# First heads' q and k written by column-tile matmuls straight into the padded layout

## The chip, the cores and the metric

One core of a Trainium2 chip. The time is device microseconds of one execution; lower is better. The engines are named as the profile names them: PE (TensorE), DVE (VectorE), ACT (ScalarE), POOL (GpSimd), SP (SyncE, here only an issuer of transfers).

## The reference

Two layers, A and B, run twice in turn over x of 2048 tokens by 640 features, all bfloat16. B is a feed-forward layer. A is causal attention inside four segments of 512 tokens, with 32 heads of 20 features, mixed with a linear-attention memory that runs over the segments.

```python
def _A_ref(x, wq, wk, wv, wo, beta):
    ...
    phi = lambda t: jnp.where(t > 0, t + 1.0, jnp.exp(t))
    g = _sigmoid(beta).reshape(1, H, 1, 1)
    ...
    for s in range(N):
        qs, ks, vs = (q[:, :, s].copy(), k[:, :, s].copy(), v[:, :, s].copy())
        logits = jnp.einsum('bhqd,bhkd->bhqk', qs, ks) * scale + mask
        p = _softmax(logits, axis=-1)
        a_dot = jnp.einsum('bhqk,bhkd->bhqd', p, vs)
        pq = phi(qs)
        num = jnp.einsum('bhld,bhde->bhle', pq, M)
        den = jnp.einsum('bhld,bhd->bhl', pq, z)[..., None] + 1e-06
        a_mem = num / den
        outs.append(g * a_mem + (1.0 - g) * a_dot)
        pk = phi(ks)
        M = M + jnp.einsum('bhld,bhle->bhde', pk, vs)
        z = z + jnp.einsum('bhld->bhd', pk)
    ...
x = x + _A_ref(_layernorm(x, axis=-1), A_wq, A_wk, A_wv, A_wo, A_beta)
x = x + _B_ref(_layernorm(x, axis=-1), B_w1, B_w2)
x = x + _A_ref(_layernorm(x, axis=-1), A_wq, A_wk, A_wv, A_wo, A_beta)
x = x + _B_ref(_layernorm(x, axis=-1), B_w1, B_w2)
```

## The kernel before

**A planner writes the order.** The whole program is a set of Python generators (streams), each of which yields operations, needs and acquisitions of buffers. The planner `Sched` keeps a time for each engine and always emits the operation that its own model lets start first; equal starts are decided by a priority (the number in `S.add`), with scores and exponentials at 0, v at 4, the q and k projections at 5, constants at 7 and loads at 8. Each engine then runs its instructions in that fixed order and waits on semaphores. The table `SHIFT` (from line 175) adds an offset in ns to the start that the planner compares, by stream, phase and count of operations; it changes the order and nothing else.

**TensorE modes.** A projection can be emitted in full width (line 764, 128 output features at once) or as four column tiles of 32 features (line 767). Scores are emitted in row tiles (line 1293). The planner lets a projection keep the column mode that it finds, and chooses anew only behind scores.

**The start.** x, wk and wq are loaded in pieces: the first 256 columns of wk and wq (`wk0`, `wq0`) ahead of the rest, then wv (`loads`, lines 610 to 631). The first segment has four tiles of 128 tokens; each is normalised, transposed on TensorE (`first_tile`, line 847) and copied to xnT. `proj_first` (line 982) then projects q and k by chunks of 128 features (c = 0 to 4; n = 0 is k, n = 1 is q). Chunks 0 and 1 come in three pieces, over tile 0, tile 1, and tiles 2 and 3 together (`PIECES`); chunks 2 to 4 in one piece. Each piece is copied from PSUM to `stg` (lines 971 and 972), where a feature lies on the partition of its place in the chunk.

**The padded layout.** Scores need the four heads of a group at partitions 0, 32, 64 and 96, with 20 features each. `pad` holds this for two groups (a pair, z = 0 and 1), for k and q, over 512 tokens. Usually a chunk goes from stg to scratch in HBM (`spill`, line 1047) and back from there into pad, 20 rows at a time (`fill`, line 1096). For the first pair `first_heads` (line 1065) copies rows straight from stg to pad: nine transfers, on the ACT and SP queues in turn (line 1089). The second pair needs chunks 1 and 2 through the scratch.

**Scores to output.** A pair has five rounds of two halves. Each half is a batch of score matmuls (line 1293) and an exponential on ACT over 128 x 1024 (line 1357); POOL then applies the causal selection (line 1369), and TensorE multiplies with v (line 1389). Four pairs make a segment, 40 exponentials.

**Other pieces that the change touches.** `late_loads` (line 633) loads the x tiles of the third segment (`x2..`, line 637) once the first pair's transfers are issued. `consts` (line 679) builds `maskg`, which picks the blocks of heads in the memory update: selections on POOL, then five multiplications by gate values on DVE (line 727). `phi_` (line 1117) frees or transforms the stg slots. It needs k of chunk 0 in stg; q of the first segment is never transformed.

Of the kernel before, what the change touches and what calls it, by code (L numbers as in the profile page):

```python
# [12 lines left out]
DH = 20  # L13
# [146 lines left out]
class Spawn:  # L160
# [345 lines left out]
def bass_interleave_layers__memory_aug_infini_attn__dense_activation_relu__prompt_kernel(  # L506
    nc, A_x, A_wq, A_wk, A_wv, A_wo, A_beta, B_x, B_w1, B_w2, out,
):
    with contextlib.ExitStack() as es:
# [438 lines left out]
        def proj_part(a, s, c, n, h):  # L948
# [29 lines left out]

            yield Spawn(5, settle())
            return tk  # L980

        def proj_first():
            order = [(c, n, h) for h in range(len(PIECES)) for c in range(2) for n in range(2)]
            order += [(c, n, None) for c in range(2, FC) for n in range(2)]
# [752 lines left out]
```

## Time and profile before

| | us |
|---|---|
| Three runs | 550.38, 552.99, 553.38 (median 552.99) |
| The profiled execution | 550.77 |
| Its span in the profile | 548.3 |
| First score matmul, first exponential | 17.97, 18.40 |

A line of the profile gives the start and the length in us, the engine, the line of the kernel, the operation, and out<-in by the program's names; `x5` means five instructions in a row; square brackets hold the idle time just before and what ended it. "SPq" and "ACTq" are those engines' queues when they issue transfers. "PEld" is the loading of weights on TensorE, which overlaps the matmuls. In tables of stretches each engine has its busy time with the count of instructions, followed by the granted TensorE clock, the DMA share and GB/s. In grouped lines the two numbers behind the bar are the summed busy time in us and the mean ns of one instruction. In lists of waits the three numbers are us in total, times, and the longest.

### The profile page before, as it was taken

How to read it: one execution, taken by the hardware profiler on the slowest of the kernel's cores; microseconds unless marked ns; L12 is line 12 of the kernel's file. 1: busy time of each engine (PE TensorE's matmuls, PEld its weight loads, DVE VectorE, ACT ScalarE, POOL GpSimd, SP SyncE). 2: the span in 40 equal slices, each digit the busy share in tenths (PEclk: the TensorE clock that was granted, in tenths of full speed). 3: DMA queues.
4: the chain of work that ended last, by engine and by line, in shares of the span. 5: the costliest groups of instructions: out<-in, count | busy, mean ns of one | idle time of the engine just before them, and what ended most of it. 6: DMA issues, size and time to landing. Idle time of an engine off the chain costs nothing.

```text
span 548.3 us, 22987 instructions
## 1 busy us (share of the span) xinstructions
PE 540.1 (99%) x10283; PEld 309.9 (57%) x10283; DVE 424.7 (77%) x1060; ACT 409.9 (75%) x522; POOL 196.8 (36%) x305
## 2 busy tenths in 40 slices
PE   8999999999999999999999999999999999999997
PEld 7434465455554555545465554665456655657766
DVE  4999898798889789987798887989688877637102
ACT  6899979899878898788888878886787776551140
POOL 2655533343444334343344444334333322301000
PEclk9999999999999999999999999999999999999999
DMA  8799789845635326375384614571265611340401
GB/s 272 189 231 259 162 179 203 222 86 105 164 83 89 78 39 163 78 114 77 115 144 114 110 31 140 115 126 26 52 179 102 122 34 28 80 83 15 88 4 51
DMA packets 133476, 62.36 MB, mean 114 GB/s; under 512 B 112258, under 2 KB 123266, under 8 KB 133378
## 3 DMA queue, kind: packets, MB, share of 16 engines
q1 hardware_dynamic: 132832, 60.38, 50.8%
q8 instruction: 81, 1.33, 1.0%
q10 hardware_dynamic: 546, 0.52, 0.3%
q14 instruction: 17, 0.14, 0.1%
HBM read 20.57 MB, written 12.85 MB: 61 GB/s over the span
## 4 chain that ended last, share of the span: by engine, by line
PE 89%; DVE 4%; DMA 4%; POOL 1%; ACT 1%; SPq 1%; issue 1%
PE ps L767 48%; PE ps L764 22%; PE ps L1293 9%; PE ps L1389 6%; PE ps L1172 2%; DMA scr<-stg 1%; DMA x_sb<-in_A_x_dram 1%; PE ps L1230 1%; DMA otk<-otu 1%; PE ps L1564 1%; ACT PT L1357 1%; DVE stats L785 1%; POOL PT L1369 1%; SPq L615 0%; POOL rstd L801 0%
## 5 line engine op out<-in xcount | busy, mean ns | idle before, releaser
L1357 ACT ACTIVATE PT<-ps 128x1024 bf16<-128x1024 f32 x320 | 309.3, 1023 | 61.6 <-PE ps L1293 57.6
L1369 POOL TENSOR_SCALAR_AFFINE_SELECT PT<-PT 128x512 bf16<-128x512 bf16 x256 | 169.9, 681 | 247.6 <-ACT PT L1357 247.6
L767 PE MATMUL ps<-xnT,w_r 128*32 128x512 bf16 x1856 | 110.9, 379 | 0.0
L767 PE MATMUL ps<-w_r,hT 128*32 128x320 bf16 (+1 forms) x1876 | 72.7, 295 | 0.0
L767 PEld LDWEIGHTS ps<-xnT,w_r 128*32 128x32 bf16 x1856 | 46.7, 97 | 44.6 <-issue 5.0
L1293 PE MATMUL ps<-pad 20*128 20x512 bf16 (+3 forms) x1024 | 63.3, 301 | 0.0
L764 PE MATMUL ps<-w_r,hT 128*128 128x320 bf16 x376 | 60.3, 300 | 0.0
L1606 DVE TENSOR_TENSOR x_sb<-x_sb,ps 128x320 bf16<-128x320 bf16 (+1 forms) x65 | 30.7, 475 | 37.8 <-PE ps L767 35.6
L785 DVE BATCH_NORM_STATS2 stats<-x_sb 128x6 f32<-128x320 bf16 x124 | 55.2, 474 | 3.9 <-DMA x_sb<-in_A_x_dram 3.3
L767 PEld LDWEIGHTS ps<-w_r,hT 128*32 128x32 bf16 x1876 | 47.9, 97 | 12.4 <-issue 1.6
L1293 PEld LDWEIGHTS ps<-pad 20*128 20x128 bf16 x1024 | 17.8, 92 | 51.1 <-issue 25.0
L764 PEld LDWEIGHTS ps<-w_r,hT 128*128 128x128 bf16 x376 | 34.7, 98 | 17.5 <-issue 5.0
L1587 ACT ACTIVATE hT<-ps 128x512 bf16<-128x512 f32 x52 | 31.1, 598 | 17.9 <-PE ps L767 17.3
L1586 DVE TENSOR_SCALAR hT<-ps 128x512 bf16<-128x512 f32 x52 | 35.3, 680 | 11.7 <-PE ps L767 9.0
L1511 DVE TENSOR_TENSOR x_sb<-x_sb,ps 128x320 bf16<-128x320 bf16 x64 | 30.1, 478 | 15.5 <-PE ps L767 12.1
L801 POOL TENSOR_TENSOR rstd<-lnU,mhalf 128x2 f32<-128x2 f32 (+2 forms) x27 | 21.0, 778 | 56.2 <-DVE lnU L797 42.8
L1389 PE MATMUL ps<-PT,v_aug 128*21 128x128 bf16 (+3 forms) x896 | 40.3, 300 | 0.0
L1399 DVE CAST otu<-ps 128x512 bf16<-128x512 f32 x50 | 34.1, 683 | 7.9 <-PE ps L1389 7.6
L971 DVE CAST stg<-ps 128x512 bf16<-128x512 f32 x42 | 28.5, 683 | 8.4 <-PE ps L767 7.1
L1483 DVE TENSOR_TENSOR o_sb<-otk,rden 128x320 bf16<-128x320 bf16 x62 | 33.9, 571 | 0.6
L831 DVE TENSOR_SCALAR xn_tok<-x_sb,mv,rstd 128x640 bf16<-128x640 bf16 x60 | 29.8, 519 | 3.4 <-POOL rstd L801 3.4
L1138 ACT ACTIVATE stg<-stg 128x512 bf16<-128x512 bf16 x50 | 31.6, 631 | 0.4 <-DVE rtmp L1136 0.4
(113 smaller groups left out, 706.7 us busy)
## 6 DMA issues: line engine op xcount, KB each, us to landing
pad<-scr SPq DMA_DIRECT2D x124, 80.0 KB
scr<-stg SPq DMA_DIRECT2D x34, 256.0 KB, 2.6
out_dram<-x_sb SPq DMA_DIRECT2D x15, 160.0 KB, 2.2
w_r<-in_B_w_dram SPq DMA_DIRECT2D x10, 216.0 KB, 3.8
w_r<-in_B_w_dram SPq DMA_DIRECT2D x13, 160.0 KB, 2.9
x_sb<-in_A_x_dram SPq DMA_DIRECT2D x10, 160.0 KB, 3.3
scr<-w_r SPq DMA_DIRECT2D x5, 256.0 KB, 4.0
wv_r<-in_A_wv_dram SPq DMA_DIRECT2D x1, 800.0 KB, 7.7
```

What stands on the lines that cost most here:

```text
L764: return e.matmul(view(dst.ap, b), a, b, start=(k == 0), stop=(k == last))
L767: return e.matmul(view(dst.ap[rows], b), part, b, start=(k == 0), stop=(k == last))
L785: tk = yield dve(320, 1, lambda e, c2=c2: e.bn_stats(stats6[:, t, c2, :], x_sb[:, t, c2 * 320:(c2 + 1) * 320]), xt)
L1138: te = yield act(512, lambda e, q=q: e.activation(q, q, ACT.Exp), [tr] + p, psum=False)
L1293: fns.append([(lambda e, z=z, j=j, hh=hh, N=N, o=o, sl=sl, q=hh % 2: e.matmul(slot.ap[:, q, o:o + N], sl.ap[32 * hh:32 * hh + DH, z, 0, 12 ...
L1357: tx = yield act(1024, lambda e, dst=dst, src=src: e.activation(dst, src, ACT.Exp, scale=SCALE), sc + pw)
L1369: tm = yield pool(600.0, lambda e, reg=reg: e.affine_select(out=reg, in_=reg, pattern=[[0, 4], [1, 128]], compare_op=ALU.is_ge, fill=0.0, ...
L1389: fns.append((lambda e, OD, j=j, hh=hh: e.matmul(OD.ap[32 * hh:32 * hh + DH + 1, 128 * j:L], VAUG[vx(a, s)][:, j, 4 * g + hh, :], pt.ap[:, ...
L1399: te = yield evac(L, 1, lambda e: e.tensor_copy(dst, OD.ap), lambda e: e.activation(dst, OD.ap, ACT.Copy), [tk] + OTU[0].tks)
L1483: to = yield dve(320, 1, lambda e, z=z, dst=dst: e.tensor_tensor(dst, av[:, z, :, :, 0:DH], rd.ap[:, z].to_broadcast([128, NJ, 4, DH]), AL ...
L1586: th = yield evac(512, 1, lambda e: e.tensor_scalar(hT[:, dc, :], bk.ap[:, :], 0.0, None, ALU.max), lambda e: e.activation(hT[:, dc, :], b ...
L1587: lambda e: e.activation(hT[:, dc, :], bk.ap[:, :], ACT.Relu), [tk] + HT.tks)
```

## The change

Four things change together.

1. k and q of the first eight heads (groups z = 0 and 1) are no longer projected as chunk 0 and copied. A new generator, `padded_part`, projects one group over two tiles: for each of the five blocks of input features, four column-tile matmuls, one a head, each with 32 columns of the weights from the head's first on. The four results lie at partitions 0, 32, 64 and 96 of one PSUM bank, and one copy takes all 128 partitions to pad. The 12 columns above a head's 20 belong to neighbouring heads; nothing reads those rows. There are eight such parts (two groups, k and q, two halves of the tokens).
2. Chunk 1 is still projected to stg, its first two pieces ahead of the padded parts and the third behind them. k of chunk 0 is copied back from pad to stg by seven transfers on SP, q of chunk 0 isn't kept in stg at all, and pad's release waits for the copies back.
3. The third segment's x comes in two transfers on SP right behind wv and beta, instead of four single tiles among the late loads.
4. The masks' memset and selections stand earlier in the stream of constants (ahead of the need of the second pair of normalised tiles), and the five multiplications by the gates go from DVE to POOL. All offsets in `SHIFT` are new (some 260 entries).

```diff
 SHIFT = {
-    (0, 0, 0): -12, (0, 1, 1): -26, (0, 2, 0): -50, (0, 3, 0): -50, (1, 0, 0): -312, (1, 0, 1): -1663,
...
+    (0, 0, 0): -12, (0, 0, 1): -62, (0, 3, 0): -50, (0, 4, 1): -25, (1, 0, 0): 50, (1, 0, 1): -100, (1, 0, 2): -550,
...
 }
@@ loads, behind wv and beta
+            for i in range(0, NJ, 2):
+                t = 2 * NJ + i
+                tk = yield dma("sp", sem_("d_x2%d" % (i // 2)), 327680, lambda e, t=t: e.dma_start(
+                    x_sb[:, t:t + 2, :], xs[:, t:t + 2, :]), lat=2000.0)
+                for k in range(2):
+                    S.set("x2%d" % (i + k), tks=[tk])
@@ late_loads
-            pieces = x_pieces(2)
-            pieces += [rows("wo", wo_r, A_wo, k) for k in range(FC)]
+            pieces = [rows("wo", wo_r, A_wo, k) for k in range(FC)]
@@ consts
-                tm = yield dve(140, 1, lambda e, mc=mc, h0=h0, h1=h1: e.tensor_tensor(
-                    mc, mc, gt[:, 2, h0:h1][:, :, None].to_broadcast([128, h1 - h0, DH]), ALU.mult), [tg] + tmm, port=True)
+                tm = yield pool(500, lambda e, mc=mc, h0=h0, h1=h1: e.tensor_tensor(
+                    mc, mc, gt[:, 2, h0:h1][:, :, None].to_broadcast([128, h1 - h0, DH]), ALU.mult), [tg] + tmm)
@@ new, ahead of proj_first
+        HALF = ((0, 2), (2, 4))
+
+        def padded_part(z, n, h, ev):
+            w_r, nm = ((wk_r, "wk0"), (wq_r, "wq0"))[n]
+            xt = yield Need("xts", 0, 0)
+            xt = xt[0]
+            sl = yield Need("pad00")
+            sl = sl[0]
+            w = yield Need(nm)
+            t = yield Need("xt", 0, 0, h)
+            i0, i1 = HALF[h]
+            t0, N = 128 * i0, 128 * (i1 - i0)
+            bk = None
+            for k in range(FC):
+                fns = [(lambda e, b=None, bk=bk, k=k, hh=hh: e.matmul(
+                    (b or bk).ap[32 * hh:32 * hh + 32, 0:N].rearrange("p (i n) -> p i n", n=128),
+                    w_r[:, k, 80 * z + DH * hh:80 * z + DH * hh + 32], feat(xt, k)[:, i0:i1],
+                    start=(k == 0), stop=(k == FC - 1)), k == FC - 1 and hh == 3) for hh in range(4)]
+                if k == 0:
+                    bk, tk = yield pe(mm_ns(N), fns, w + t, acq=MISC, mode="cols")
+                else:
+                    tk = yield pe(mm_ns(N), fns, mode="cols")
+
+            def settle():
+                dst = sl.ap[:, z, n, t0:t0 + N]
+                te = yield evac(N, 1, lambda e: e.tensor_copy(dst, bk.ap[:, 0:N]),
+                                lambda e: e.activation(dst, bk.ap[:, 0:N], ACT.Copy), [tk] + sl.tks)
...
+                if len(ev) == 4:
+                    S.set("pad", 0, 0, z, tks=[sl] + [x for _, x in ev])
+                    S.set("padk", z, tks=[x for y, x in ev if y == 0])
...
@@ proj_first
-            order = [(c, n, h) for h in range(len(PIECES)) for c in range(2) for n in range(2)]
-            order += [(c, n, None) for c in range(2, FC) for n in range(2)]
...
+        ORDER = [(1, n, h) for h in range(2) for n in range(2)]
+        ORDER += [(z, n, h) for z in (-1, -2) for h in range(2) for n in range(2)]
+        ORDER += [(1, n, 2) for n in range(2)] + [(c, n, None) for c in range(2, FC) for n in range(2)]
@@ first_heads
-                        tk = yield dma(("act", "sp")[turns % 2], sem, 2048 * (rb - ra), lambda e, p0=p0, ra=ra, rb=rb, c=c, z=z: e.dma_start(
-                            sl.ap[p0:p0 + rb - ra, z], stg[ra - 128 * c:rb - 128 * c, c]), ev + sl.tks, issue=720.0, lat=2200.0, rate=200.0)
...
+            S.set("pad00", tks=[sl])
+            back = yield Acq([STG[0][0][0]])
+            sem = sem_("first")
+            for z in range(2):
+                ev = yield Need("padk", z)
+                for hh in range(4):
+                    ra = 80 * z + 20 * hh
+                    rb = min(ra + DH, 128)
+                    if ra < rb:
+                        tk = yield dma("sp", sem, 1024 * (rb - ra), lambda e, ra=ra, rb=rb, z=z, hh=hh: e.dma_start(
+                            stg[ra:rb, 0, 0], sl.ap[32 * hh:32 * hh + rb - ra, z, 0]), ev + back.tks,
+                            issue=720.0, lat=2200.0, rate=200.0)
+            S.set("direct", 0, tks=[tk])
@@ scores, at the end of a pair
-                        pads[m].release(tk)
+                        back = (yield Need("direct", 0)) if m == 0 else []
+                        pads[m].release(tk, *back)
```

In `ORDER`, -1 and -2 stand for the padded groups z = 0 and 1, and the three numbers are chunk or group, k or q, and the piece.

More of the change, by code (lines that the diff above doesn't have):

```diff
@@ L689, in consts @@
             S.set("mhalf", tks=[th])
+            ntk = yield Need("normed", 3)
+            t3 = yield pool(700, lambda e: e.memset(maskg[:], 1.0), ntk)
+            tmm = []
+            for c in range(FC):
+                h0, h1 = CH_H0[c], CH_H1[c]
+                mc = maskg[:, CH_OFF[c]:CH_OFF[c + 1]].rearrange("p (h e) -> p h e", e=DH + 1)
+                t5 = yield pool(400, lambda e, mc=mc, n=h1 - h0, base=128 * c - DH * h0: e.affine_select(
+                    out=mc, in_=mc, compare_op=ALU.is_ge, fill=0.0, base=base,
+                    pattern=[[-DH, n], [0, DH + 1]], channel_multiplier=1), [t3])
+                tm = yield pool(400, lambda e, mc=mc, n=h1 - h0, base=DH - 1 + DH * h0 - 128 * c: e.affine_select(
+                    out=mc, in_=mc, compare_op=ALU.is_ge, fill=0.0, base=base,
+                    pattern=[[DH, n], [0, DH + 1]], channel_multiplier=-1), [t5])
+                tmm.append(tm)
             yield Need("xt", 0, 0, 1)
@@ L980, in proj_part @@
             return tk
-        def proj_first():
-            order = [(c, n, h) for h in range(len(PIECES)) for c in range(2) for n in range(2)]
-            order += [(c, n, None) for c in range(2, FC) for n in range(2)]
-            for z, (c, n, h) in enumerate(order):
-                if z >= 1:
-                    c0, n0, h0 = order[z - 1]
-                    yield Need("qkpart", 0, 0, c0, n0, h0)
-                tk = yield from proj_part(0, 0, c, n, h)
+        HALF = ((0, 2), (2, 4))
@@ new lines, in proj_first @@
+        def proj_first():
+            evs = [[], []]
+            order = ORDER
+            for i, (c, n, h) in enumerate(order):
+                if i >= 1:
+                    c0, n0, h0 = order[i - 1]
+                    yield Need("padpart", -1 - c0, n0, h0) if c0 < 0 else Need("qkpart", 0, 0, c0, n0, h0)
+                if c < 0:
+                    tk = yield from padded_part(-1 - c, n, h, evs[-1 - c])
+                else:
+                    tk = yield from proj_part(0, 0, c, n, h)
```

45 lines of the change are left out of this document (8 added, 37 removed), and 86 rows, old and new, of the table SHIFT.

## Prediction

> **What bounds the kernel now.** I began with the page: how busy each engine is, and the chain that ended last.
>
> ```profile
> span 548.3 us, 22987 instructions
> PE 540.1 (99%) x10283; PEld 309.9 (57%) x10283; DVE 424.7 (77%) x1060; ACT 409.9 (75%) x522; POOL 196.8 (36%) x305
> PE 89%; DVE 4%; DMA 4%; POOL 1%; ACT 1%; SPq 1%; issue 1%
> ```
>
> TensorE carries 89% of the last chain and is busy 99% of the span. That average hides a start with other limits, and the change acts only there. So the second view was the table of busy time by stretch, and for the middle two stretches the same table of the exponentials alone (line 1357).
>
> ```profile
> core 0: us, PE busy (x) PEld busy (x) DVE busy (x) ACT busy (x) POOL busy (x), PEclk, DMA share, GB/s
> 8.00:13.00 5.00, 4.46 (x65) 4.08 (x63) 2.97 (x7) 2.92 (x10) 0.74 (x2) 1.00 1.07 351
> 13.00:18.00 5.00, 4.79 (x34) 2.63 (x32) 4.00 (x17) 2.10 (x7) 0.00 (x0) 1.00 0.39 97
> 18.00:30.00 12.00, 12.00 (x109) 5.88 (x112) 11.53 (x30) 11.40 (x15) 9.66 (x18) 1.00 0.96 218
> 30.00:61.00 31.00, 28.65 (x430) 12.45 (x419) 28.98 (x68) 29.78 (x33) 17.67 (x27) 1.00 0.92 239
> 61.00:548.00 487.00, 484.33 (x9606) 279.48 (x9603) 373.60 (x930) 358.38 (x449) 165.48 (x246) 1.00 0.48 99
> ...
> 18.00:30.00 12.00, 8.54 (x9) 1.00 0.96 218
> 30.00:61.00 31.00, 29.36 (x32) 1.00 0.92 239
> ```
>
> Read it downwards. From 13 to 18 us ScalarE works 2.10 of 5 us. From 18 to 30 everything is full: PE 12.00 of 12, DVE 11.53, ACT 11.40. From 30 to 61 ACT does almost nothing but exponentials (29.36 of 31 us), DVE is at 28.98, and PE misses 2.35 us. After 61 PE is idle for 2.67 us in 487. So what happens up to 61 us decides when PE becomes the only limit; behind that, an earlier start is an earlier end, and additional TensorE work is a later one.
>
> The third view, the order in time, shows why the exponentials start only at 18.4 us.
>
> ```profile
> 10.76 0.49 DVE L867 COPY xnT<-ps 128x640 bf16<-128x640 bf16 x1 [0.62 <-PE ps L856]
> ...
> 11.40 0.71 PE L764 MATMUL ps<-xnT,wk_r 128*128 128x256 bf16 x5
> ...
> 11.94 0.71 PE L764 MATMUL ps<-xnT,wq_r 128*128 128x256 bf16 x5
> ...
> 12.49 0.71 PE L764 MATMUL ps<-xnT,wk_r 128*128 128x256 bf16 x5
> 12.69 0.38 ACT L972 ACTIVATE stg<-ps 128x256 bf16<-128x256 f32 x1 [0.16 <-PE ps L764]
> ...
> 13.10 3.15 SPq L1089 DMA_DIRECT2D pad<-stg  x4
> 13.10 1.33 ACTq L1089 DMA_DIRECT2D pad<-stg  x1
> ...
> 17.97 0.40 PE L1293 MATMUL ps<-pad 20*128 20x512 bf16 x4
> ...
> 18.40 1.94 ACT L1357 ACTIVATE PT<-ps 128x1024 bf16<-128x1024 f32 x2
> ```
>
> The last of the four normalised tiles is in place at 11.25 (10.76 + 0.49). The first chunk of q is out of PSUM at 13.07 (12.69 + 0.38). Then transfers carry rows from stg to pad, and the first score waits until 17.97: 4.9 us in which the data only moves to other partitions.
>
> **The transfers removed: -4.8 us.** The new first group is also k then q over 256 tokens, placed right after the same tile, so I give it the times of the rows at 11.40, 11.94 and 12.69. It writes pad itself, ready at 13.07, and with 0.1 us for the signal (the transfers followed within 0.03) the score starts near 13.2 instead of 17.97. ACT also gets its queue back: it issued four of the transfers, the first taking 1.33 us.
>
> **Column tiles added: +2.2 us of TensorE.** A group's price is the distance between starts, since the ends overlap.
>
> ```profile
> 9.09 0.44 PE L764 MATMUL ps<-xnT,wq_r 128*128 128x128 bf16 x5
> ...
> 9.37 0.44 PE L764 MATMUL ps<-xnT,wk_r 128*128 128x128 bf16 x5
> ...
> 13.58 1.24 PE L764 MATMUL ps<-xnT,wk_r 128*128 128x512 bf16 x5
> ...
> 46.78 1.26 PE L767 MATMUL ps<-hT,wq_r 128*32 128x512 bf16 x20
> ```
>
> Five matmuls over 128 tokens take 0.28 us (9.37 - 9.09), over 256 tokens 0.55 (12.49 - 11.94), so 1.1 over 512. Twenty column-tile matmuls over 512 take 1.26 us where five full ones take 1.24: the same price for a quarter of the output columns times four. The eight new parts cost 8 x 0.55 = 4.4; the first chunk that they replace cost 4 x 0.28 + 2 x 0.55 = 2.2. The 2.2 more lie before 30 us, where PE has no gap to hide them. Bounds: 0 if the gaps left before 18 us (0.54 + 0.21 visible in the table, and waits shorter than a matmul's overhang) take most of it, and 2.2.
>
> **Changes of tiling mode: +0.9 us.** A part in column tiles stands between full-width groups. The nearest price is the weight load's idle time behind a batch of scores, which also changes the tiling:
>
> ```profile
> 30.62 0.40 PE L1293 MATMUL ps<-pad 20*128 20x512 bf16 x4
> 30.94 0.10 PEld L764 LDWEIGHTS ps<-hT,wk_r 128*128 128x128 bf16 x1 [0.23 <-issue]
> ```
>
> 0.23 us each. The eight parts are consecutive in their stream and the planner lets a full-width projection stay in the column mode that it finds, so I take two visits, four changes: 0.9. Bounds 0 and 16 x 0.23 = 3.7. The Trainium skill speaks against the change here: "TensorEngine Tiling (Array Packing)", section Key Properties, says that changing the tiling mode, unlike changing the tile, drains TensorE. The row above agrees for score batches; no row shows the change from full width to column tiles alone. By that rule with every part alone the sum is rival C below.
>
> **Evacuations and masks: -1.1 us.**
>
> ```profile
> 9.57 1.12 ACT L972 ACTIVATE stg<-ps 128x128 bf16<-128x128 f32 x4 [0.99 <-PE ps L764]
> ...
> L727 DVE TENSOR_TENSOR maskg<-maskg,gt 128x140 bf16<-128x140 bf16 x4 | 2.0, 488 | 0.0
> ...
> L727 DVE TENSOR_TENSOR maskg<-maskg,gt 128x160 bf16<-128x160 bf16 x1 | 0.3, 319 | 0.0
> ...
> 46.37 1.06 DVE L1257 TENSOR_TENSOR BD<-M_sb,maskg 128x462 bf16<-128x462 f32 x1
> ...
> PEld ps L767 <- DVE w_r L971: 1.4, 2, 0.9
> ```
>
> Eight evacuations of 0.38 replace four of 0.28 (1.12 / 4) and two of 0.38: 3.0 - 1.9 = +1.2 us on ACT or DVE. The five multiplications of the masks leave DVE, where they took 2.0 + 0.3 = 2.3 us, all of it between 30 and 61 us. In that stretch PE waits for DVE's evacuations, up to 0.9 us at once, so DVE's time is paid: I take the difference, -1.1. Bounds -2.3 (ACT's freed queue absorbs the evacuations) and +1.2 (the exponentials alone pace the stretch). On GpSimd the masks are covered: it is idle 13 us of the 31 and nothing needs the masks before the memory update at 46.37. Without that cover each would stand before a causal selection.
>
> **Third x loads, transfers back: 0.** Two loads go to SP's queue behind wv, out of the place where they stand between the first two spills:
>
> ```profile
> 17.76 0.92 SPq L637 DMA_DIRECT2D x_sb<-in_A_x_dram  x2
> 17.79 0.59 ACT L972 ACTIVATE stg<-ps 128x512 bf16<-128x512 f32 x1
> ...
> 18.72 0.43 SPq L1060 DMA_DIRECT2D scr<-stg  x1
> 19.19 0.93 SPq L637 DMA_DIRECT2D x_sb<-in_A_x_dram  x2
> ...
> 22.84 0.66 SPq L1109 DMA_DIRECT2D pad<-scr  x1
> ...
> 25.94 1.17 SPq L1109 DMA_DIRECT2D pad<-scr  x3
> ...
> scr<-stg SPq DMA_DIRECT2D x4, 256.0 KB, 3.0
> ...
> L1089 SPq DMA_DIRECT2D pad<-stg x5: 668/722/910, 13.1 to 16.3; - x5
> ```
>
> That clears 1.85 us of SP and of transfer time before the second pair's pad. Against it stand seven transfers from pad back to stg, 0.72 us of SP each as the median of the old ones: 5.0 us after 13 us, on SP alone, with the first spill, the normalised tiles' transposes and the second pair's fill queued behind. SP is otherwise free until the third chunk is projected, which now happens later; that covers them. Bounds -1.1 (a spill landing in 3.0 rather than about 4.1 us, from 18.72 to the fill at 22.84) and +1.4 (5.0 against the 5 x 0.72 = 3.6 that SP issued before).
>
> **New offsets: 0.** They reorder all that follows. After 61 us PE's visible idle time is 2.67 us; that is all that a better order could take from there by the table, and I allow a worse one as much.
>
> The sum: 550.77 (the profiled execution's own time; span 548.3 and 2.5 around it) - 4.8 + 2.2 + 0.9 - 1.1 = 548.0 us. The runs shown have a median of 552.99, 2.2 above that execution; two of the three lie near 553, so the same effect on those would end near 550.
>
> A check speaks for modesty. PE's visible idle time from 8 to 61 us is 0.54 + 0.21 + 0 + 2.35 = 3.1 us. To take in 3.1 us more work and still end 2.8 earlier, 5.9 us of lost TensorE time must go, so about half of it has to come out of waits that hide under the modelled ends of matmuls (each PE record reaches 0.71 - 0.55 = 0.16 us past the next start).
>
> **The rivals.**
>
> A, the whole head start arrives. The parts of the second group and the second chunk fill gaps while ACT works on the first scores, and the spill lands quicker: 550.77 - 4.8 - 1.1 - 1.1 = 543.8. For it: ACT's 2.9 idle us from 13 to 18 and a DVE that loses 2.3. Against it: PE full from 18 to 30.
>
> B, slower: the third feature chunk comes late. The second pair of heads needs chunks 1 and 2 through scr, and now behind the first score stand four parts of the second group (2.2), the rest of chunk 1 (1.1), chunk 2 (2.2), and between them score batches with their changes of mode (some 2.2) and, since v has the better priority, up to eight v groups of 320 columns (8 x 0.68 = 5.5, scaled from 0.55). 13.2 + 13.2 = 26.4, its evacuation 27.0, spill 3.0, four fills 1.6 (1.17 / 3 each), landing 3.0: 34.6 against 30.62 now. Exponentials would stall 4.0 us: 554.8. It decides from chunk 2 leaving PSUM after 30.62 - 7.6 = 23.0 us. Now it does so at 18.4 (17.79 + 0.59), and the planner sees this wait, which speaks against the full price.
>
> C, no gain: every part pays two changes of mode, 3.7 instead of 0.9, and the sum is 550.77 - 4.8 + 2.2 + 3.7 - 1.1 = 550.8.
>
> **How the numbers follow.** The forecast has 0.38, with 545.5 to 550.5 as its own range (its small bounds together); A 0.26, B 0.24, C 0.12. About 0.5%, 2.8 us, is what a measurement of this kernel can tell from no change. The forecast lies on that line, slightly past it: I split it 0.21 faster, 0.17 same. A is faster. C is same but for 0.02. B is slower but for 0.02. Faster 0.21 + 0.26 = 0.47; same 0.17 + 0.10 + 0.02 = 0.29; slower 0.22 + 0.02 = 0.24. The range reaches from A with part of what a better order could take (542.5) to B with 1.2 for the evacuations (556).
>
> **What would show it.** The first score near 13.2 us and the first exponential at 13.6. The second pair's first score near 28.9 (30.62 - 4.8 + 2.2 + 0.9); before 27 speaks for A, after 31 for B. The fortieth exponential, now in the stretch that ends at 61 us, near 58. PE's idle time from 30 to 61 below 2.35 if DVE's relief counts. Idle time of about 0.23 before each column-tile part would be C. The forecast is wrong if the first score starts on time and the second pair doesn't follow, or if the difference arises after 61 us, where only the order has changed.

## The result and the profile after

The changed kernel takes 554.84 us (median of five runs, 554.40 to 555.36), the kernel before 552.51 in the runs beside it (550.38 to 553.38). The ratio is 1.0062 with a 95% interval of [1.0044, 1.0080]: slower, by 2.4 to 4.4 us. The two medians lie 2.3 us apart, a little less than that. Repeated later on one chip with other runs (e17 below) the ratio was 1.0047 [1.0032, 1.0062], 2.6 us. So the loss is some 3 us, and the 3.4 us of the first ratio are used below. The forecast was 548.0.

The page of the changed kernel, the lines on the span, on busy time and on the chain that ended last:

```profile
span 552.9 us, 22830 instructions
PE 543.6 (98%) x10200; PEld 312.0 (56%) x10200; DVE 423.6 (77%) x1048; ACT 413.3 (75%) x531; POOL 196.7 (36%) x310
PE 88%; ACT 6%; DVE 2%; DMA 2%; POOL 1%; issue 1%
```

The span is 4.6 us longer, more than the median difference, because the profiled run of before was a short one (550.77, with a median of 552.51). Of the 4.6, TensorE is busy for 3.5 (543.6 - 540.1), and 1.1 is more idle time. ACT has 6% of the last chain in place of 1%.

The early order in time, after (the new parts are line 1002, their copy on ACT line 1014; scores are now line 1331, exponentials 1396):

```profile
9.65 0.44 PE L769 MATMUL ps<-xnT,wq_r 128*128 128x128 bf16 x5
10.03 0.73 PE L1002 MATMUL ps<-xnT,wk_r 128*32 128x256 bf16 x20
10.69 0.45 PE L861 MATMUL ps<-om_sb,xn_tok 128*128 128x128 bf16 x5
11.07 0.73 PE L1002 MATMUL ps<-xnT,wq_r 128*32 128x256 bf16 x20
...
13.26 0.38 ACT L1014 ACTIVATE pad<-ps 128x256 bf16<-128x256 f32 x1 [0.16 <-PE ps L1002]
13.70 0.39 PE L1331 MATMUL ps<-pad 20*128 20x512 bf16 x4
...
14.03 0.73 PE L1002 MATMUL ps<-xnT,wq_r 128*32 128x256 bf16 x20
14.13 1.94 ACT L1396 ACTIVATE PT<-ps 128x1024 bf16<-128x1024 f32 x2
...
14.58 0.60 PE L1002 MATMUL ps<-xnT,wk_r 128*32 128x256 bf16 x13
...
16.63 0.40 PE L1002 MATMUL ps<-xnT,wk_r 128*32 128x256 bf16 x7 [1.45 <-issue]
...
25.39 0.68 DVE L976 CAST stg<-ps 128x512 bf16<-128x512 f32 x1
26.09 0.33 SPq L1110 DMA_DIRECT2D scr<-stg  x1
...
28.23 1.44 SPq L1145 DMA_DIRECT2D pad<-scr  x4
...
34.31 0.39 PE L1331 MATMUL ps<-pad 20*128 20x512 bf16 x4
...
34.74 1.02 ACT L1396 ACTIVATE PT<-ps 128x1024 bf16<-128x1024 f32 x1
```

The first score starts at 13.70 instead of 17.97, the first exponential at 14.13 instead of 18.40: the transfers are gone and 4.3 us are won. A part takes 0.55 us (14.58 - 14.03), just as priced. But TensorE stops for 1.45 us in the middle of the seventh part, waiting for nothing that the profile names. Chunk 2 is out of PSUM at 26.07 (25.39 + 0.68; before 18.38), and the second pair's first score comes at 34.31; before it was at 30.62. The 4.3 us have become a later second pair.

The table by stretch, first after, then before, with the stretch from 30 to 140 us cut finer than in the prediction:

```profile
8.00:13.00 5.00, 4.60 (x115) 3.69 (x116) 2.73 (x8) 2.82 (x8) 3.53 (x10) 1.00 1.08 353
13.00:18.00 5.00, 3.55 (x112) 2.62 (x104) 3.85 (x13) 3.13 (x6) 3.25 (x7) 1.00 0.56 177
18.00:30.00 12.00, 12.00 (x101) 6.59 (x95) 10.67 (x30) 11.19 (x18) 3.73 (x6) 1.00 0.66 170
30.00:36.00 6.00, 6.00 (x63) 2.57 (x61) 4.96 (x15) 3.51 (x7) 3.11 (x7) 1.00 0.71 173
36.00:61.00 25.00, 23.99 (x306) 10.05 (x306) 16.66 (x30) 25.00 (x28) 14.87 (x24) 1.00 0.74 188
...
66.00:140.00 74.00, 72.43 (x955) 40.17 (x953) 68.69 (x176) 63.97 (x87) 26.46 (x41) 1.00 0.72 163
140.00:300.00 160.00, 159.97 (x2872) 88.08 (x2871) 138.56 (x342) 134.26 (x161) 67.18 (x101) 1.00 0.54 107
```

```profile
30.00:36.00 6.00, 4.98 (x75) 1.79 (x64) 5.53 (x14) 4.92 (x7) 3.03 (x5) 1.00 0.92 244
36.00:61.00 25.00, 23.67 (x356) 10.67 (x355) 23.45 (x55) 24.86 (x27) 14.64 (x23) 1.00 0.92 238
...
66.00:140.00 74.00, 74.00 (x1051) 40.05 (x1050) 64.68 (x162) 65.81 (x87) 27.57 (x42) 1.00 0.72 162
```

Three things changed. From 13 to 18 us PE lost 1.24 us (3.55 for 4.79). From 30 to 61 it won 1.34 (29.99 for 28.65), and ACT fell to 3.51 of 6 us between 30 and 36, the hole ahead of the second pair. From 66 to 140, where PE was full before, it is idle for 1.57 us (1.26 in the profile of e17, the same kernel again); DVE has 4.0 us more to do there and 6.8 less between 36 and 61.

Busy time doesn't tell which work was done. So I also added up, for both traces, the columns that TensorE still has to stream after a given moment, at 0.42 ns a column (1.08 us for five matmuls over 512 columns, rows with e1 below), with a fourth of that for matmuls that run four at a time (column tiles, scores). Records are missing in both traces, so a difference is good to about 0.5 us. In the changed kernel this remaining work is larger by 4.2 us at 18 us, by 2.3 at 36, by 2.2 at 61, by 4.3 at 116 and by 4.8 at 300. The extra columns of the new parts are work of its own and lie ahead of 18 us. So the kernel is 2.2 us behind when the first stage ends, and loses 2.1 more between 61 and 116 us.

### The profile page after: what moved, and what is told of

Read it like the earlier page. It is cut to its first block, busy times and chain, and to the rows that moved or that the text cites. A ratio compares the mean times of both kernels' runs of the same rounds, so it can differ in the third digit from the quotient of the medians.

```text
span 552.9 us, 22830 instructions
## 1 busy us (share of the span) xinstructions
PE 543.6 (98%) x10200; PEld 312.0 (56%) x10200; DVE 423.6 (77%) x1048; ACT 413.3 (75%) x531; POOL 196.7 (36%) x310
## 4 chain that ended last, share of the span: by engine, by line
PE 88%; ACT 6%; DVE 2%; DMA 2%; POOL 1%; issue 1%
PE ps L772 46%; PE ps L769 24%; PE ps L1331 8%; PE ps L1428 6%; ACT PT L1396 6%; PE ps L1210 2%; DMA phk<-phs 1%; PE ps L1268 1%; PE ps L1002 1%; PE ps L1603 1%; DVE xn_tok L836 1%; POOL rstd L806 1%; DMA x_sb<-in_A_x_dram 0%; DVE stats L790 0%; DVE otu L1438 0%
## 5 line engine op out<-in xcount | busy, mean ns | idle before, releaser
L1408 POOL TENSOR_SCALAR_AFFINE_SELECT PT<-PT 128x512 bf16<-128x512 bf16 x256 | 167.9, 674 | 244.7 <-ACT PT L1396 244.5
L772 PE MATMUL ps<-xnT,w_r 128*32 128x512 bf16 x1724 | 105.4, 380 | 0.0
L772 PEld LDWEIGHTS ps<-xnT,w_r 128*32 128x32 bf16 x1724 | 42.5, 97 | 40.6 <-issue 6.1
L769 PE MATMUL ps<-w_r,hT 128*128 128x320 bf16 x381 | 62.1, 300 | 0.0
L976 DVE CAST stg<-ps 128x512 bf16<-128x512 f32 x50 | 34.1, 684 | 6.5 <-PE ps L769 3.5
L772 PE MATMUL ps<-wo_r,oT 128*32 128x320 bf16 x788 | 33.2, 300 | 0.0
L1428 PEld LDWEIGHTS ps<-PT,v_aug 128*21 128x21 bf16 x896 | 21.7, 92 | 19.3 <-POOL PT L1408 1.7
```

What stands on the lines that cost most here:

```text
L769: return e.matmul(view(dst.ap, b), a, b, start=(k == 0), stop=(k == last))
L772: return e.matmul(view(dst.ap[rows], b), part, b, start=(k == 0), stop=(k == last))
L976: te = yield evac(N, 1, lambda e: e.tensor_copy(sg.ap[:, t0:t0 + N], bk.ap[:, 0:N]), lambda e: e.activation(sg.ap[:, t0:t0 + N], bk.ap[:, ...
L1408: tm = yield pool(600.0, lambda e, reg=reg: e.affine_select(out=reg, in_=reg, pattern=[[0, 4], [1, 128]], compare_op=ALU.is_ge, fill=0.0, ...
L1428: fns.append((lambda e, OD, j=j, hh=hh: e.matmul(OD.ap[32 * hh:32 * hh + DH + 1, 128 * j:L], VAUG[vx(a, s)][:, j, 4 * g + hh, :], pt.ap[:, ...
```

## The experiments

The order of both kernels comes from a planner, and any edit reshuffles it. For experiments on one part, the order was therefore written out as a list of the planner's choices, and the list was followed with that one edit (line numbers are then some 100 higher). Ratios are against the kernel before, run on the same chip; one per cent is 5.5 us.

| | edit | median us | ratio, 95% interval |
|---|---|---|---|
| e1 | before, chunks 3 and 4 twice | 556.61 | 1.0089 [1.0065, 1.0113] |
| e16 | after, chunks 3 and 4 twice | 558.75 | 1.0125 [1.0109, 1.0141] |
| e15 | before, less work at the front | 553.35 | 1.0026 [1.0015, 1.0037] |
| e9 | after, less work at the front | 555.15 | 1.0061 [1.0038, 1.0083] |
| e17 | after itself, beside e15 and e16 | 554.88 | 1.0047 [1.0032, 1.0062] |
| e2 | after, fewer TensorE instructions | 556.19 | 1.0085 [1.0064, 1.0105] |
| e3 | after, x2 loads later | 555.48 | 1.0076 [1.0054, 1.0098] |
| e12 | the same again | 555.22 | 1.0061 [1.0040, 1.0081] |
| e7 | after, second pair earlier | 557.12 | 1.0104 [1.0080, 1.0128] |
| e13 | after, fourth x block earlier | 554.09 | 1.0050 [1.0032, 1.0069] |
| e4 | before, masks on GpSimd | 551.26 | 0.9999 [0.9985, 1.0012] |
| e8 | before, x2 loads early | 551.23 | 0.9996 [0.9976, 1.0016] |
| e10 | after with the old offsets | 604.42 | 1.0954 [1.0922, 1.0987] |
| e11 | before with the new offsets | 600.18 | 1.0889 [1.0845, 1.0934] |
| e5 | before without offsets | 566.50 | 1.0280 [1.0254, 1.0307] |
| e14 | e5 with x2 loads early | 562.03 | 1.0197 [1.0172, 1.0222] |
| e6 | after without offsets | 565.58 | 1.0259 [1.0233, 1.0285] |

### Is added work at the front paid?

```diff
             bk, tk = yield from group(MISC, N, [...], w)
+            if (a, s) == (0, 0) and c in (3, 4):
+                for k in range(FC):
+                    tk = yield pe(mm_ns(N), [(lambda e, k=k: e.matmul(
+                        bk.ap[:, 0:N].rearrange(...), w_r[:, k, c * 128:(c + 1) * 128], ...
```

> The kernel before, with its own order of instructions written out as a list, and one addition: the k and q projections of the fourth and fifth chunk of the first segment (128 features each) run twice into the same bank, the second pass overwriting the first. That is 4 groups of five 128x512 matmuls, 4 x 1.07 = 4.3 us more TensorE work between 20 and 32 us, and nothing else. Theory W (TensorE is full from 8 us on, so every added us of its work is a later end): 4 to 4.5 us slower than before. Rival I (the start has idle TensorE time that added work can fill, as the forecast had it): at most 2 us slower.

A group and its repetition, in TensorE's order in time of that kernel (lines 864 and 1072):

```profile
18.41 1.24 PE L864 MATMUL ps<-xnT,wk_r 128*128 128x512 bf16 x5
19.49 1.24 PE L1072 MATMUL ps<-xnT,wk_r 128*128 128x512 bf16 x5
```

They start 1.08 us apart. Four such groups, 4.3 us of TensorE ahead of 36 us, made the kernel before 4.9 us slower (3.6 to 6.2). In the time the work is paid in full. It isn't simply passed on, though: by the remaining work this kernel is only 2.3 us behind at 36 us and 2.1 at 61, and the rest of the delay comes later.

> The changed kernel with chunks 3 and 4 of the first q and k projected twice, its order held: 4.3 us more TensorE work between 20 and 36 us, the mirror of e1. Theory R and theory W: 4 to 5.5 us above the changed kernel. If the changed kernel had room there that the first kernel hasn't: under 2.5 us above it.

The same edit in the changed kernel: 3.9 us by the medians of e16 and e17 (558.75 - 554.88), 4.3 by their ratios. It is paid there too, at the low end of what was expected.

### The pause at 15 us

```diff
-            tk = yield pe(107.0 * 41, [(warm_mm, k == 40) for k in range(41)], [tw])
+            tk = yield pe(107.0 * 41, [(warm_mm, k == 9) for k in range(10)], [tw])
...
-                yield pe(380.0, [(warm_mm, False) for _ in range(5)])
+                yield pe(380.0, [(warm_mm, False) for _ in range(1)])
```

> The changed kernel in its own order, with the warm-up of TensorE made of 11 matmuls over 512 columns in place of 46 over 128: the same streamed columns, 70 TensorE instructions fewer ahead of the pause that its trace shows at 15.18 us (1.45 us, waited for nothing shown). Theory F (TensorE ran out of loaded instructions; the next block of 16 KB had landed only at 15.48): the pause comes some 70 instructions later and shrinks below 1 us; if the pause costs the end, the time falls by 0.5 to 1 us against after (554.84). Rival D (the pause is a data dependence): it stays 1.45 us at the same matmul.

Only the matmuls that warm the clock up were made fewer and wider (31 and 4 fewer), which takes 70 instructions from TensorE with their weight loads. TensorE's order in time in that kernel:

```profile
15.03 0.72 PE L1102 MATMUL ps<-xnT,wq_r 128*32 128x256 bf16 x20
15.58 0.39 PE L872 MATMUL ps<-xnT,wk_r 128*32 128x256 bf16 x8
17.37 0.51 PE L872 MATMUL ps<-xnT,wk_r 128*32 128x256 bf16 x12 [1.39 <-issue]
```

The pause has moved from behind the 13th of a part's 20 matmuls to behind the 8th of the group after the next: 7 + 20 + 8 = 35 matmuls, 70 instructions with their weight loads. It sits at a count of instructions, so it isn't a wait for data. The profile's table of queues has one for instructions, q8; this is its line for the changed kernel, for transfers that start between 13 and 14.4 us.

```profile
q8 instruction: 1, 0.02, 4.8%
```

One block of 16 KB (0.02 MB here) moves from 14.12 to 15.18 in the changed kernel, and TensorE resumes at 16.63, 1.45 behind it (the expectation's 15.48 is 0.30 too late). In e2 the block is there at 16.09, 0.9 us later, and TensorE resumes at 17.37, 1.28 behind it; so the pause didn't shrink below 1 us, as theory F had it. In e13 it is there at 14.67, TensorE resumes at 15.97, 1.30 behind it, and the pause is 0.83. The fixed count and the steady distance say that TensorE has run out of instructions: twenty small matmuls and twenty weight loads for 0.55 us use them up faster than five and five do. That this block holds TensorE's instructions is inferred from this. The time isn't lower.

For the next run only the order list is changed: the two loads of the third x block, 320 KB each, go out later.

```diff
 order of SP
-     9.11  x_sb<-in_A_x_dram  x2
...
      stg<-pad  x2
+    16.33  x_sb<-in_A_x_dram  x2
      stg<-pad  x5
```

> The changed kernel in its own order, with only the two transfers of the third x moved from behind beta (issued at 9.11 us) to between the second and the third transfer back from pad to stg (about 14.6 us). Theory F with x2 as the cause (the block of instructions waits behind x): the block lands about 2 us sooner and the pause at 15.18 goes; 1 to 1.5 us faster than after if the pause is paid. Rival: the block still starts near 14.4 behind wv, the pause stays, and the time is after's 554.8 or up to 1 us more.

The block is there at 14.48, and the pause is gone. The time isn't lower. The granted clock in this profile was 0.50 from 9 to 12 us, which hides what the pause was worth, so the kernel ran again:

> The kernel of e3_after_x2_later once more, for a second profile, since the first one showed a granted clock of 0.50 from 9 to 12 us. Theory P (the pause of 1.4 us is paid, and only the clock hid it): with a clock of 1.00 at 9 to 12 us the span is 1 to 1.5 us under that of the changed kernel (552.9), near 551.5. Theory F (what the parts win is waited for behind them): with a clock of 1.00 the span is still 552.5 to 554, and the median 554.5 to 556.

Theory F's median came (555.22; the ratio is 1.0061 beside the changed kernel's 1.0062). The clock fell again, so the condition of both theories wasn't met. In this profile's table by stretch, and then in TensorE's order in time (the seventh part, which had the pause):

```profile
8.00:9.00 1.00, 1.00 (x11) 0.86 (x10) 0.85 (x2) 0.00 (x0) 0.80 (x3) 0.50 1.09 327
9.00:10.00 1.00, 1.00 (x12) 1.00 (x11) 0.65 (x2) 0.28 (x1) 0.00 (x0) 0.50 1.08 335
10.00:11.00 1.00, 1.00 (x11) 0.86 (x9) 0.20 (x1) 0.55 (x2) 0.73 (x1) 0.52 1.08 366
```

```profile
15.60 0.80 PE L1102 MATMUL ps<-xnT,wk_r 128*32 128x256 bf16 x20
```

Here the first number behind "1.00," is PE's busy time and the one ahead of the DMA share the clock: 0.50, 0.50, 0.52. With the slow clock TensorE comes to the seventh part late, at 15.60 (16.04 in e3) instead of 14.58, and the block, there at 14.55, is in time for that. Had it come there at 14.58, a block at 14.5 and a distance of 1.3 us would have left about 0.6 us of the pause (an estimate from the rows above). Nor is it shown that the loads hold the block up: with them early it is there between 14.65 (e16) and 15.31 (e17), without them at 14.48 and 14.55. So the price of the pause by itself stays open. What can be said is that the two sets of six runs with this order are no faster.

### Does an earlier second pair help (rival B)?

Only the order list is changed:

```diff
 order (start of the second pair's pieces, us)
-     chunk 2, q: evacuation 25.39, spill 26.09, fills 28.23; scores 34.31
+     chunk 2, q: spill 23.16, fills 26.68; scores 31.55, ahead of chunk 4's projections
```

> The changed kernel with a list of its order in which the q part of chunk 2, its spill and its fills, and then the second pair's scores stand some places earlier, so that these scores start near 31 us instead of 34.3; the work is the same. Rival B (the late second pair is what costs): 3 us earlier scores give 551 to 552.5 us. Theory W (TensorE is never without work between 18 and 36 us, so that what goes first only pushes other work behind it, and the hole in ScalarE's row moves to the third pair): second pair near 31 us and still 554.5 to 558 us.

TensorE's rows of scores in this kernel (line 1431):

```profile
31.55 0.40 PE L1431 MATMUL ps<-pad 20*128 20x512 bf16 x4
...
37.11 0.40 PE L1431 MATMUL ps<-pad 20*128 20x384 bf16 x8
```

The second pair starts at 31.55, 2.8 us earlier, and the kernel is slower still: 5.7 us above before (4.4 to 7.1), where the changed kernel has 3.4. The batch behind it comes only at 37.11. By the remaining work it is 3.2 us behind before at 36 us instead of 2.3. The new list also brings waits of its own: TensorE is idle for 2.65 us between 18 and 66 us, for 1.28 in the changed kernel. So rival B's gain didn't come, but what the late second pair costs by itself isn't shown.

### Does less work at the front help?

```diff
             bk = None
-            for k in range(FC):
+            for k in range(3):
...
-                    start=(k == 0), stop=(k == FC - 1)), k == FC - 1 and hh == 3) for hh in range(4)]
+                    start=(k == 0), stop=(k == 2)), k == 2 and hh == 3) for hh in range(4)]
```

> The changed kernel with the padded column parts built from three of the five blocks of features instead of all five (q and k of the first eight heads are partial sums, so the output differs), the rest of its order held. It takes 8 x 2/5 x 0.55 = 1.8 us of work from TensorE between 10 and 18 us. Theory W (each us of work is paid, wherever it lies): 552.6 to 553.6 us. Theory F (at the front TensorE isn't the bound in this kernel; what comes behind the parts is late by itself and the hole moves there): 554.3 to 556 us, with the 1.8 us found again as idle time of TensorE before 62 us.

The ratio is the changed kernel's own. Theory F holds: 1.8 us less work gains 0.1 us, with about 1.6 either way. The pause is gone here too: the eight parts run through, and the second batch of scores, at 18.05 in the changed kernel, starts at 15.31. The table by stretch:

```profile
18.00:30.00 12.00, 11.30 (x81) 5.80 (x80) 9.92 (x28) 9.23 (x15) 4.04 (x7) 1.00 0.75 176
30.00:36.00 6.00, 4.55 (x62) 1.69 (x60) 4.23 (x14) 3.49 (x5) 2.97 (x6) 1.00 0.99 181
```

And TensorE's order in time, that batch and around 33 us:

```profile
15.31 0.40 PE L1431 MATMUL ps<-pad 20*128 20x384 bf16 x8 [0.39 <-ACT PT L1496]
...
32.33 0.40 PE L1431 MATMUL ps<-pad 20*128 20x512 bf16 x4
...
34.71 0.39 PE L869 MATMUL ps<-hT,wq_r 128*128 128x512 bf16 x1 [1.45 <-DVE w_r L1076]
```

The second pair starts 2.0 us earlier (32.33), and then TensorE waits 1.45 us for a copy on DVE. Between 18 and 36 us it is idle for 2.15 us (0.70 + 1.45) where the changed kernel has none. By the remaining work it is 2.6 us ahead of the changed kernel at 18 us, 0.2 at 36 and level at 300. So neither the work nor the pause, taken out together, is worth anything at the end of this order. Is that the changed kernel's own, or any fixed order's? The mirror in the kernel before, with the same three blocks in chunks 0 and 1:

```diff
-                (w_r[:, k, c * 128:(c + 1) * 128], feat(xt, k)[:, i0:i1]) for k in range(FC)], w)
+                (w_r[:, k, c * 128:(c + 1) * 128], feat(xt, k)[:, i0:i1]) for k in range(3 if (a, s) == (0, 0) and c < 2 else FC)], w)
```

> The kernel before with chunks 0 and 1 of the first q and k built from three of the five blocks of features (partial sums, so the output differs), its order held: 4 x 1.08 x 2/5 = 1.7 us less work for TensorE between 8 and 17 us, the mirror of e9. Theory W (each us at the front is paid): 549 to 550 us, 1.3 to 2 us under the kernel before. Theory R (a fixed order is a ratchet: it passes delays on and keeps savings as idle time, in both kernels): within 0.8 us of the kernel before, with the 1.7 us found again as idle time before 36 us.

It is slower than before by 1.4 us (0.8 to 2.0). R comes nearest, and even it didn't expect a loss. The saving is gone early. TensorE comes to the first group of v 1.0 us sooner and waits there for v's weights, until 14.81; in before that group starts at 15.04 after 0.21 us of such a wait:

```profile
14.81 0.84 PE L864 MATMUL ps<-wv_r,xnT 128*128 128x320 bf16 x5 [1.03 <-DMA wv_r<-in_A_wv_dram]
```

By the remaining work the kernel is 1.7 us ahead at 8 us and level with before at 18, so the idle time lies ahead of 36 us, as R said. The first score starts at 17.75 instead of 17.97. The loss comes on top, first between 36 and 61 us, and 0.95 us of new idle time follows between 66 and 140. The second line is from the list of TensorE's waits:

```profile
36.00:61.00 25.00, 22.03 (x332) 9.85 (x331) 22.98 (x51) 23.40 (x26) 14.45 (x23) 1.00 1.02 237
PE ps L864 <- DVE stats L885: 1.6, 1, 1.6
```

22.03 instead of 23.67 in before's row above: 1.6 us more waiting, which is that one wait. In both kernels, then, added work at the front is paid in the time (e1, e16) and a saving there isn't passed on (e9, e15). What stops a saving is what the next instruction of the fixed order still waits for: v's weights in e15, a copy on DVE in e9. Theory R's word ratchet names this, but no run shows one single mechanism behind it.

> The changed kernel itself beside the two runs above, on the same chip: 1.0044 to 1.008 of the kernel before, as measured.

The repetition gave 1.0047 [1.0032, 1.0062].

### The loss between 61 and 116 us

In before the loads of the fourth block of x go out at 37.84 and 40.84, and the eight statistics of its normalisation run between 49 and 58 us (the ninth of the line below is the third block's last). In the changed kernel the four loads go out together at 61.62, and the eight run behind that, in the stretch where eight others run in both kernels. SP's rows of these loads and, in the grouped lines of DVE from 36 to 61 and from 61 to 116 us, the statistics, all in before:

```profile
37.84 1.38 SPq L637 DMA_DIRECT2D x_sb<-in_A_x_dram  x2
40.84 1.34 SPq L637 DMA_DIRECT2D x_sb<-in_A_x_dram  x2
```

```profile
L785 DVE BATCH_NORM_STATS2 stats<-x_sb 128x6 f32<-128x320 bf16 x9 | 4.0, 462 | 0.0
L785 DVE BATCH_NORM_STATS2 stats<-x_sb 128x6 f32<-128x320 bf16 x8 | 3.5, 482 | 0.0
```

The same in the changed kernel, the statistics from 61 to 116 us:

```profile
61.62 2.47 SPq L643 DMA_DIRECT2D x_sb<-in_A_x_dram  x4
```

```profile
L790 DVE BATCH_NORM_STATS2 stats<-x_sb 128x6 f32<-128x320 bf16 x16 | 7.5, 473 | 0.0
```

The edit moves these loads and statistics forward in the order list.

```diff
 order
-     x_sb<-in_A_x_dram  x4 at 61.62, stats<-x_sb behind 66
+     x_sb<-in_A_x_dram  at 36.80, 43.54, 48.88, 52.32, stats<-x_sb between them and 67
```

> The changed kernel with a list of its order in which the loads of the fourth block of x go out from about 36 to 52 us instead of at 61.6, and the statistics of its normalisation stand between 43 and 67 us instead of after 66; the work is the same and the rest of the order is held. Theory L (these statistics, pushed to where VectorE is full, make TensorE idle between 66 and 140 us): TensorE's busy time there rises from 72.4 towards 74.0 and the time is 552.5 to 553.7 us. Theory D (VectorE's load there isn't what TensorE waits for; the waits are single chains of the order): idle time there within 0.4 us of 1.6, time 554.5 to 557 us.

TensorE's stretch in this kernel:

```profile
66.00:140.00 74.00, 73.18 (x974) 40.53 (x976) 66.12 (x168) 64.52 (x88) 27.26 (x42) 1.00 0.74 162
```

Idle time falls from 1.57 (1.26 in e17) to 0.82 us and DVE's work there from 68.69 to 66.12. Between 61 and 116 us the remaining work falls behind by 1.1 us, in the changed kernel by 2.1 and in e17 by 1.8. But other runs with the late fourth block lose between 1.3 (e16) and 2.7 us (e2) there. The time, 2.8 us above before (1.8 to 3.8), is 0.7 under the changed kernel's, within both intervals, and no lower than its repetition's ratio. L's time (552.5 to 553.7) wasn't reached, D's (554.5 to 557) neither, and the idle time left D's bound. That the late fourth block carries up to 1 us of this loss is likely and not shown. The longest wait that stayed is one chain of the memory's turn; this is the line among the waits of the changed kernel, and the one here is as long:

```profile
PE ps L1428 <- DVE rmem L1224: 0.7, 1, 0.7
```

### The parts that were forecast at nothing, or as a gain

```diff
-                tm = yield dve(140, 1, lambda e, mc=mc, h0=h0, h1=h1: e.tensor_tensor(
+                tm = yield pool(500, lambda e, mc=mc, h0=h0, h1=h1: e.tensor_tensor(
```

> The kernel before in its own order, with only the five multiplications of the masks computed on GpSimd instead of VectorE (the selections stay where they are). The forecast (VectorE's time is paid between 30 and 61 us): 1 to 2.3 us faster than before. Theory W: no faster; up to 1 us slower where the multiplications stand before causal selections.

Nothing, within 0.8 us. DVE's 2.3 us weren't paid: in this trace TensorE is idle 0.4 us less than in before from 30 to 36 us, and 0.7 more from 36 to 61.

```diff
+                tk = yield dma("sp", sem_("d_x2%d" % (i // 2)), 327680, ...   # behind wv and beta
...
-            pieces = x_pieces(2)
-            pieces += [rows("wo", wo_r, A_wo, k) for k in range(FC)]
+            pieces = [rows("wo", wo_r, A_wo, k) for k in range(FC)]
```

> The kernel before with the four loads of the third block of x put behind wv as in the change, the rest of its order held. Theory W: no difference, 550.5 to 553 us (within 0.3% of the kernel before). Rival: these 1.3 MB ahead of later loads delay a transfer that the first 30 us need, 1 to 3 us more.

Nothing, within 1.3 us. (The four tiles are 160 KB each, 0.66 MB in all, not 1.3.)

### The offsets

The edit is the table alone: the other kernel's table in e10 and e11, and none in e5, e6 and e14.

```diff
-SHIFT = {
...
+SHIFT = {}
```

> The change without one of its parts: the changed kernel with the table of offsets of the kernel before. Theory O (an offset belongs to the one order that it was chosen in): far slower, 575 to 600 us. The forecast's term for the new offsets (0, at most 2.7 us either way) says 552 to 558 us.

> The kernel before with the new table of offsets and nothing else of the change. Theory O: far slower, 575 to 600 us. The forecast's term for the offsets: 548 to 556 us.

Either table in the other kernel costs some 50 us, at or a little beyond the upper end of theory O's range. In the profile of e10 TensorE is idle for 45.1 us (600.9 - 555.8) instead of 9.3, and for 34 us the granted clock was 0.50; in e11 it was for 41 us. An offset isn't a property of a stage; it belongs to the one sequence in which it was found. So the orders were compared without any.

> The kernel before with an empty table of offsets (SHIFT = {}), everything else as it was. Read beside the next run. The offsets were chosen for one structure each, so both kernels should lose without them: some 8 to 18 us here (560 to 571 us).

> The changed kernel with an empty table of offsets. Theory W (TensorE has nothing to give, so the work and the pause that the column parts add are paid in any order): 2.2 to 4.6 us above the run without offsets before it. Theory O (the parts are worth something, and what loses is the order that the new offsets give): level with that run or 1 to 3 us below it.

The gap closes: 565.58 against 566.50, their intervals overlap. As stated, that is theory O; the 566.50 lie where they were expected. But the run that adds the loads alone divides it:

> The kernel of e8 (third x loads behind wv) with an empty table of offsets, to be read beside the two runs without offsets. Theory O (in an order that wasn't tuned, an early load is room that the order uses; in the tuned one it isn't): 1 to 4 us under the 566.5 us of the kernel before without offsets. Theory W (the loads are off the path in any order): 565.5 to 567.5 us.

Without offsets the early loads gain 4.5 us (566.50 - 562.03), somewhat more than theory O's 1 to 4, and what else the change has (column parts, masks, copies back) costs 3.5 (565.58 - 562.03). The runs were on two chips; by the ratios it is 4.6 and 3.4. Both rest on one order each, and a planner's orders scatter, so the sizes are rough; the signs lie outside the intervals. With offsets the early loads gain nothing in before's order (e8), perhaps because that order was made for late ones.

No run was faster than the kernel before.

## Why the prediction was wrong

**The transfers removed, -4.8: the step that failed.** The first score came 4.3 us earlier, near the forecast, and the forecast booked that as an earlier end. Its own rule, "behind that, an earlier start is an earlier end", is what fell. TensorE has a fixed amount of work, so it ends earlier only by idle time that goes. Its idle time from 8 to 61 us was 3.1 us before and is 2.9 after (5.00 - 4.60, 5.00 - 3.55, 0, 0 and 25.00 - 23.99 in the table): in place of 4.8 us, 0.2 went. With 2.2 us of work added, that leaves it 2.0 us behind; by the remaining work it is 2.2 at 61 us. The pause in the seventh part, 1.45 us of this idle time, is new and was not foreseen. Nor is a saving at the front passed on: 1.8 us in e9 and 1.7 us in e15 came back as idle time before 36 us, and e7 moved the second pair by 2.8 us for a slower kernel. The paragraph that spoke for modesty had the warning: the visible idle time was 3.1 us, and the waits assumed beneath the matmuls' modelled ends didn't show up in this sum.

**Column tiles, +2.2.** The size was right (0.55 us a part). Full-width groups added behind 18 us are paid in the time (e1, e16). That taking a part of the work away again gains nothing (e9) shows that the terms can't simply be added or taken off one by one.

**Changes of mode, +0.9.** Too large. From 9.65 to 10.03 and from 10.69 to 11.07 it is 0.38 us, where five matmuls over 128 columns take 0.28, and from 10.03 to 10.69 it is 0.66, where a part takes 0.55. So a change between full width and column tiles cost about 0.1 us here, not 0.23, and there are three ahead of the first score. Consecutive parts follow each other in 0.55 us without one. Rival C's time (550.8) and its sign of 0.23 before each part didn't come.

**Evacuations and masks, -1.1.** The masks' share, -2.3, is zero in the time (e4). The evacuations' share, +1.2, wasn't tested by itself.

**Third x loads, transfers back: 0.** Zero for the loads in before's order (e8). Missed was that in an order that may use them they are worth 4.5 us (e14 against e5). The transfers back took 6.9 us of SP (13.13 to 20.00) instead of 5.0. No run tests them alone; TensorE has no idle time from 18 to 36 us that could be theirs.

**New offsets, 0 with 2.7 either way.** Not a term at all: e10 and e11 show 49 to 53 us for a table in the wrong kernel. The idle time after 61 us was taken as all that an order could win or lose there; the changed order added 1.57 us in a stretch that had none.

**Rival B** named the place and nearly every number: chunk 2 out of PSUM at 26.07, past its point of 23.0; the second pair at 34.31 against 34.6; 554.8 us against 554.84. Its reason for that time was only partly right, so the last match is in part luck. The stall it priced at 4.0 us is 3.7 at the twelfth exponential (35.7 for 32.0 us) and 1.5 at the fortieth (61.0 for 59.6), and taking 2.8 us of it away gained nothing (e7). About half of the loss came later, by the forecast's own last sign: "if the difference arises after 61 us". By the remaining work 2.2 of 4.8 us are there at 61 us and the rest follows.

**What stays open.** The 3.4 us are not divided to the end. Shown are that added TensorE work is paid, that the head start isn't passed on, and that some 2 us of the remaining work are lost by 61 us. The 2 us after that are seen and not explained; the late fourth block may carry up to 1 of them. How much a better order of the changed kernel could still win, and what the column parts alone would cost in an order tuned for them, wasn't tried on the chip.

## What to carry to other kernels

Where the busiest engine is at 99%, ask first how much idle time it has ahead of the point at which it becomes the only limit; that sum, and not the length of the wait that is removed, was what could be gained here. In an order that is fixed, test an early stage both ways, with work added and with work taken away: if only the first shows in the end, look for what the next instruction in the order waits for before you count a saving. Offsets or hand-set priorities belong to one sequence, so compare structures also without them.

## What the hardware showed unexpectedly

TensorE seems to run out of instructions. In the dense column parts it stood still for 0.83 to 1.45 us, at a fixed count of instructions, until 1.28 to 1.45 us after a 16 KB block had arrived on the instruction queue (the changed kernel, e2, e7, e13, e16 and e17). The pause was 1.45 us with the block at 15.18 and 0.83 us with the block 0.51 us earlier (e13).

A change between full width and column tiles cost TensorE about 0.1 us (0.38 us for 0.28 of matmuls, 0.66 for 0.55).

The granted clock was 0.50 for 3.4 us, from 7.5 (e12) or 9.0 us (e3) on, in both profiles of the kernel with the x2 loads late, and 1.00 there in every other profile. No run here shows why, and the times of the two don't stand out from the changed kernel's.
